# Two interleaved linear-attention and squared-ReLU layers on one core: key sums a tile later, and softmax, weight splits and a norm queued behind the work beside them

## The chip, the cores and the metric

The kernel runs on one core of a Trainium2 chip. The metric is the device time of one launch in microseconds (us). The engines are named as the profile names them: PE (TensorE, matrix products), DVE (VectorE), ACT (ScalarE), POOL (GpSimd), SP (SyncE, which issues the DMAs). Each engine works through one queue in order, so what stands where in a queue decides who waits for whom.

## The reference, cut to what matters

```python
def _A_ref(x, wqkv, w_phi, wo):                   # S=2048, D=576, H=32 heads of 18
    q, k, v = heads of (x @ wqkv)
    pq, pk = q @ w_phi[h], k @ w_phi[h]
    phi_q = concat(softmax(pq), softmax(-pq)); phi_k = concat(softmax(pk), softmax(-pk))
    kv = einsum("bhsf,bhsd->bhfd", phi_k, v); z = phi_k summed over s
    o = (phi_q @ kv) / (phi_q @ z + 1e-6)
    return o (heads joined) @ wo
def _B_ref(x, w1, b1, w2, b2):                    # F=4608
    return relu(x @ w1 + b1) ** 2 @ w2 + b2
x = A_x
for _ in range(2):
    x = x + _A_ref(layernorm(x), ...)
    x = x + _B_ref(layernorm(x), ...)
```

All values are fp32. The key sums kv and z run over all 2048 rows, so no row's attention can end before every row's keys are in.

## The kernel before

The 2048 rows are four blocks of 512 rows, each of four tiles of 128. A product in fp32 is made of three fp32r products: an operand is split into a high part (a copy by ACT) and a low part (a subtraction by DVE, a remainder by POOL). The 4608 hidden columns are 36 groups of 128.

The work is written as generators. `weave` runs one generator and advances a second one beside it by its costs; `pipeline` runs the tiles of a block through a list of stages, later stages of earlier tiles first; a stage `None` or an empty function only delays. The order written is not yet the order of the queues: a scheduler then sorts each engine's instructions by priority. `tc.issue_after(ins)` keeps what is written inside it behind `ins` on that instruction's engine, and `held(gen, keys)` does so for every step of a generator, with the instruction that `dense[key]` names at that moment: "last" is the low part of the newest hidden group (on DVE), "squared" its last square (on ACT).

Each of the two layers runs through these stages:

- Dense layer of the first block (`g_mlp`; names m_3 in the first layer, m_1 in the second), woven with the attention of another block. For each group ACT evicts the hidden product (L812), squares it (L813, L814), and PE adds the previous group's second product. The attention's softmax is `g_features`: maxima and minima on DVE, a difference on POOL (L475), the exponential on ACT (L479), sums and products for the features, scaling. Some queries (`a_1q`, L435, evicted at L453) lie here too.
- Dense layer of the second block (m_2, m_0), woven with the attention of the last two blocks, their norms (`g_norm_first`, `g_norm_second`) and the first weight splits (`prelude`).
- Products of the last two blocks together (`g_pair.products`): 18 pairs of hidden groups, each pair seven products of Strassen's kind instead of eight. In order they are a11, a12, s1, s2, s4, s3, (the second product of an earlier group), a22, another second product. The PSUM tile bx (m_ppx) takes a11, s2, s3 and a22 in one sum, which is read in between: z is the first column group (ACT L1210, DVE L1212, ACT L1213, L1121, L1122, and its low part on DVE L1123), u (DVE L1222, then L1225) and v (ACT L1221, then DVE L1226) belong to the other block and are kept in memory until later. Beside a pair the operands of a coming pair are split (`split_pair`: ACT L1069, DVE L1070, POOL L1072, and POOL's additions L1075 to L1084).
- `seconds`: the second products of the kept block, 36 groups, each fed by a weight split (L1102) and a reload of the kept values (L1187). In the first layer it is woven with `back_keys`, which makes the norm (L344 scales a tile, L355 transposes it, L364 its low part), values, keys, softmax and key sums (`kv_tile`, L527) of three blocks for the second layer. A tile's key sums need the softmax scaled by POOL (L495).

The rest is the start (`g_fold` folds w_phi into the weights, woven with the first norm), the keys of the first layer, and a `barrier` at each layer's start.

Of the kernel before, what the change touches and what calls it, by code (L numbers as in the profile page):

```python
# [21 lines left out]
def layers_kernel(  # L22
# [188 lines left out]
    def g_fold(kpair, vpair):  # L211
# [22 lines left out]
        def turn(k):  # L234
            c, i = divmod(k, 3)
            if i == 0:
                if c + 2 < NC:
                    load(c + 2)
                load_v(c)
                if c in (2, 3):  # L240
                    folds[c] = sb.tile([P, 2 * D], F32, tag="wraw", name=f"ff{c}", bufs=2)
                else:
                    folds[c] = sb.tile([P, 2 * D], F32R, tag="hb", name=f"ff{c}").bitcast(F32)
            w, n = gw[batches[i][0][1]], len(batches[i])
            pt = wtile(f"fp{c}_{i}")
# [4 lines left out]
            nc.vector.tensor_copy(wt[:w, : n * P], pt[:w, : n * P])  # L250
            return wt

        def times(k, wt):
# [414 lines left out]
    def g_features(layer, raws, ph, name):  # L668

        rs, ms = {}, {}  # L670

        def start(t):
            ph.append(soft_parts(raws[t], f"{name}Q{t}"))

        def add(t):
            rs[t] = soft_sums(ph[t], f"{name}Q{t}")
            ms[t] = phi_products(layer, ph[t], f"{name}m{t}")

        def factors(t):
            phi_factors(ms.pop(t), rs[t], f"{name}u{t}")  # L680

        yield from held(pipeline(NT, (start, lambda t: soft_exp(ph[t]), add, factors, lambda t: phi_scale(ph[t], rs[t])),
                                 (2.6, 0.4, 3.0, 2.8, 1.2)))

    def g_out(layer, b, ph, dst, name, parts=1, pause=None, behind=None, norm=None, mid=None, costs=(None, None)):

# [85 lines left out]
    def g_mlp(layer, b, x, after, name, behind=None, then=None):  # L772
# [88 lines left out]
        features(NF - 1, range(3))  # L861
        yt = sb.tile([P, TB], F32, tag="hr", name=f"{name}yt", bufs=2)
        nc.scalar.activation(yt, acc[KC], AF.Copy)
        by_rows(NF - 1, range(2), range(3))
        pt = wtile(f"{name}py")
        p3 = pt.rearrange("p (t d) -> p t d", d=P)
# [2 lines left out]
        for t in range(NT):  # L869
# [1 line left out]
            nc.sync.dma_start(x, xm[b][t])  # L871
            nc.vector.tensor_add(x[:, R:], p3[:, t], x[:, R:])
            after.append(x)
        if then:
            then()
        by_rows(NF - 1, range(2, NT), range(3))
        for t, x in enumerate(after):
            nc.vector.tensor_add(x[:, :R], acc[t][:, :R], x[:, :R])
# [3 lines left out]
    def g_norm_halves(x_of, name, then, main, tail, costs):  # L882
# [35 lines left out]
        def call(pair):  # L918
            def stage(i):
                h, j = divmod(i, 3)  # L920
                pair[j == 2](h if j == 2 else 2 * h + j, pts[i])
# [4 lines left out]
    def g_norm_first(x_of, dst, name, then):  # L926

        tiles = {}

        def main(t, p4):  # L930
            if t == 0:
                tiles.update(xt_tiles(name))
                tiles["t"] = sb.tile([P, 2 * D], F32, tag="E", name=f"{name}t", bufs=4)[:TP, : 2 * TB]
                tiles["t"] = tiles["t"].rearrange("p (a n) -> p a n", a=2)
            rows = slice(t * P, (t + 1) * P)
            hi, lo = tiles["h"][:, :KC, rows], tiles["l"][:, :, rows]
            p3 = p4.rearrange("p a c n -> p (a c) n")
            nc.scalar.activation(hi, p3, AF.Copy)
            nc.vector.tensor_sub(lo, p3, hi.bitcast(F32))

        def tail(h, p3):
            nc.scalar.activation(tiles["t"][:, :, h * TB // 2 : (h + 1) * TB // 2], p3, AF.Copy)

        yield from g_norm_halves(x_of, name, then, (main,), (tail,), (0.3, 1.0))
        nc.sync.dma_start(pth, tiles["h"][:, :KC].rearrange("p c n -> p (c n)").bitcast(F32))
        nc.sync.dma_start(ptl, tiles["l"].rearrange("p c n -> p (c n)").bitcast(F32))
        nc.sync.dma_start(ptt, tiles["t"].rearrange("p a n -> p (a n)"))
# [84 lines left out]
    def g_pair(layer, blocks, x, after, name):  # L1032
# [82 lines left out]
        def bias(f):  # L1115
            return b1t[:, f : f + 1]

        def square(f, r):
            hb = sb.tile([P, 2 * D], F32R, tag="hb", name=f"{name}hb{f}")
            hh, hl = hb[:, :TB], hb[:, TB : 2 * TB]  # L1120
            nc.scalar.activation(hh, r, AF.Square)  # L1121
            nc.scalar.activation(r, r, AF.Square)  # L1122
            nc.vector.tensor_sub(hl, r, hh.bitcast(F32))  # L1123
            high[f] = (hh, hl)

        def features(f, ks):
            b, g = divmod(f, NF)
# [72 lines left out]
        def products():  # L1200
            for k in range(NP):
# [9 lines left out]
                product(k, by, "a12", "b21", True)  # L1211
                nc.vector.tensor_add(z, by, z)  # L1212
                nc.scalar.activation(z, z, AF.Relu)  # L1213
                square(f0, z)
                advance(prep, 2)
                product(k, bz, "s1", "t1", True)
                advance(prep, 2)
                product(k, bx, "s2", "t2", False)
                u = sb.tile([P, D], F32, tag="qk", name=f"{name}u{f0}", bufs=5)[:, :TB]
                v = sb.tile([P, D], F32, tag="qk", name=f"{name}u{f1}", bufs=5)[:, :TB]  # L1220
                nc.scalar.activation(v, bz, AF.Copy)  # L1221
                nc.vector.tensor_add(u, bx, v)  # L1222
                product(k, by, "s4", "b22", True)
                product(k, bx, "s3", "t3", False)
                nc.vector.scalar_tensor_tensor(u, by, bias(f0), u, op0=ALU.add, op1=ALU.add)  # L1225
                nc.vector.scalar_tensor_tensor(v, bx, bias(f1), v, op0=ALU.add, op1=ALU.add)  # L1226
# [4 lines left out]
                if k:  # L1231
                    second(f0 - 1)
                load_wide(f1)
                advance(prep, 2)
                if k == 0:
                    yield
                product(k, bx, "a22", "t4", False)
                drain(prep)
                z = sb.tile([P, TB], F32, tag="hr", name=f"{name}z{f1}", bufs=2)
                nc.scalar.activation(z, bx, AF.Relu, bias=bias(f1))  # L1240
                square(f1, z)
                if k + 2 < NP:
                    raws[k + 2] = load_pair(k + 2)
                if k == 0:
# [80 lines left out]
    xT = [{} for _ in range(NB)]  # L1325
    kpair = [piece_tiles(f"w0k{h}", TAGS_B) for h in range(2)]
    vpair = [piece_tiles(f"w0v{h}", TAGS_A) for h in range(2)]
    weave(g_fold(kpair, vpair), g_norm(load_x(0), xT[0], "n0_0"), 0.5)
    pending = []

    def g_keys(b):
# [21 lines left out]
    for layer in range(2):  # L1353
# [23 lines left out]

        def back_keys():
            new_slots("vs")
            for b in order[:3]:  # L1380
                m = f"1_{b}"
                last = b == order[2]
                xk, vts, raws, es, rs = {}, [], {}, {}, {}
                yield from g_norm(rows_of(b), xk, f"n{m}", fine=True)
                if not last:
                    spill(b, xk)
                    yield from paced(g_v(xk, wpair("v", f"w{m}"), vts, f"v{m}"), 1.0)
# [9 lines left out]
                    rs[t] = soft_sums(es[t], f"k{m}K{t}")  # L1397
                    soft_scale(es[t], rs[t])

                stages = (raw, start, lambda t: soft_exp(es[t]), end, lambda t: None)  # L1400
                if not last:
                    stages += (lambda t: kv_tile(1, vts[t], es[t], f"kv{m}_{t}"),)
                yield from pipeline(NT, stages, (1.0, 2.6, 0.4, 1.8, 0.1, 0.8))
                if last:
                    keep.update(x=xk, es=es, v=wpair("v", f"w{m}"))

# [45 lines left out]
```

## Time and profile before

| what | value |
|---|---|
| median of 3 runs | 2559.05 us (2557.98 to 2560.22) |
| the profiled execution | 2559.82 us, its span 2558.1 us |
| mean granted TensorE clock | 0.988 |
| busy: PE, DVE, ACT, POOL | 2490.5, 1632.0, 1306.9, 967.7 us |
| DMA | 312.99 MB moved, mean 122 GB/s |

The span is the time from the first to the last instruction; 1.7 us of the profiled execution's time lie outside it. Busy times are per engine. A row of waits names the engine and tile that waited, the line, what released it, the total, how often, and the longest. A timeline row has its start, its length, the line, output and inputs, and in brackets the idle time before it with what ended it. A tile is named without its numbers in the profile (m_pu is u or v of any pair, m_ppx is bx); kv_3k<-k_3K3e is block 3, tile 3.

### The profile page before, as it was taken

How to read it: one execution, taken by the hardware profiler on the slowest of the kernel's cores; microseconds unless marked ns; L12 is line 12 of the kernel's file. 1: busy time of each engine (PE TensorE's matmuls, PEld its weight loads, DVE VectorE, ACT ScalarE, POOL GpSimd, SP SyncE). 2: the span in 40 equal slices, each digit the busy share in tenths (PEclk: the TensorE clock that was granted, in tenths of full speed). 3: DMA queues.
4: the chain of work that ended last, by engine and by line, in shares of the span. 5: the costliest groups of instructions: out<-in, count | busy, mean ns of one | idle time of the engine just before them, and what ended most of it. 6: DMA issues, size and time to landing. Idle time of an engine off the chain costs nothing. (4 is left out here: it accounts for less than half of the span.)

```text
span 2558.1 us, 41548 instructions
## 1 busy us (share of the span) xinstructions
PE 2490.5 (97%) x15108; PEld 2188.9 (86%) x15108; DVE 1632.0 (64%) x2570; ACT 1306.9 (51%) x2293; POOL 967.7 (38%) x1101
## 2 busy tenths in 40 slices
PE   8998999999999999999999989999999999999999
PEld 8998888888888888888889988888888887888888
DVE  6778847554966655555777779384658665555444
ACT  4334545354546666664443445553545466666643
POOL 3544313212325555551434433032122445555322
PEclk9998999999999999999999989999999999999999
DMA  8102432345234433338543143233453344333363
GB/s 252 57 23 88 153 92 81 107 144 187 87 116 126 138 117 101 112 102 265 178 129 115 46 138 104 80 93 107 142 175 90 125 129 144 107 103 103 110 201 128
DMA packets 257224, 312.99 MB, mean 122 GB/s; under 512 B 29818, under 2 KB 175482, under 8 KB 254458
## 3 DMA queue, kind: packets, MB, share of 16 engines
q1 hardware_dynamic: 255760, 307.64, 38.5%
q8 instruction: 118, 1.93, 0.3%
q10 hardware_dynamic: 1258, 2.70, 0.3%
q14 instruction: 88, 0.72, 0.1%
HBM read 255.42 MB, written 54.82 MB: 121 GB/s over the span
## 5 line engine op out<-in xcount | busy, mean ns | idle before, releaser
L1103 POOL TENSOR_TENSOR m_ps<-m_pr,m_ps 128x128 fp32r<-128x128 f32 x144 | 120.8, 839 | 319.8 <-ACT m_ps L1101 261.0
L1102 DVE TENSOR_TENSOR m_ps<-m_pr,m_ps 128x448 fp32r<-128x448 f32 x144 | 93.9, 652 | 152.9 <-ACT m_ps L1101 147.3
L1142 PE MATMUL m_pacc<-m_ps,m_phb 128*128 128x448 f32 x864 | 188.5, 366 | 0.0
L1142 PEld LDWEIGHTS m_pacc<-m_ps,m_phb 128*128 128x128 f32 x864 | 162.1, 188 | 18.1
L1101 ACT ACTIVATE m_ps<-m_pr 128x576 fp32r<-128x576 f32 x144 | 97.9, 680 | 132.6 <-issue 87.9
L1142 PE MATMUL m_pacacc<-m_ps,m_phc 128*128 128x448 f32 x648 | 145.7, 369 | 0.0
L1142 PEld LDWEIGHTS m_pacacc<-m_ps,m_phc 128*128 128x128 f32 x648 | 123.2, 190 | 10.1
L1123 DVE TENSOR_TENSOR m_phb<-m_pz,m_phb 128x512 fp32r<-128x512 f32 x72 | 56.5, 785 | 115.8 <-ACT m_pz L1122 114.3
L805 PE MATMUL m_1ph<-t1onh,m_1h 128*128 128x512 f32 (+1 forms) x380 | 100.3, 391 | 2.9 <-ACT m_1hr L812 2.4
L805 PE MATMUL m_3ph<-t0onh,m_3h 128*128 128x512 f32 (+1 forms) x380 | 98.6, 386 | 3.8 <-ACT m_3hr L812 2.4
L832 PE MATMUL m_2acc<-m_2s,m_2hb 128*128 128x448 f32 x432 | 100.1, 365 | 0.0
L832 PE MATMUL m_0acc<-m_0s,m_0hb 128*128 128x448 f32 x432 | 100.0, 365 | 0.0
L832 PE MATMUL m_3acc<-m_3s,m_3hb 128*128 128x448 f32 x432 | 99.7, 366 | 0.0
L832 PE MATMUL m_1acc<-m_1s,m_1hb 128*128 128x448 f32 x432 | 99.5, 365 | 0.0
L805 PE MATMUL m_0ph<-a_0nh,m_0h 128*128 128x512 f32 (+1 forms) x380 | 97.8, 384 | 0.0
L805 PE MATMUL m_2ph<-a_2nh,m_2h 128*128 128x512 f32 (+1 forms) x380 | 97.8, 384 | 0.0
L832 PEld LDWEIGHTS m_2acc<-m_2s,m_2hb 128*128 128x128 f32 x432 | 81.0, 188 | 10.6 <-ACT m_2hb L813 0.2
L832 PEld LDWEIGHTS m_0acc<-m_0s,m_0hb 128*128 128x128 f32 x432 | 81.0, 188 | 10.6 <-ACT m_0hb L813 0.2
L832 PEld LDWEIGHTS m_3acc<-m_3s,m_3hb 128*128 128x128 f32 x432 | 81.0, 188 | 10.6 <-ACT m_3hb L813 0.2
L832 PEld LDWEIGHTS m_1acc<-m_1s,m_1hb 128*128 128x128 f32 x432 | 81.0, 188 | 10.3
L805 PEld LDWEIGHTS m_1ph<-t1onh,m_1h 128*128 128x128 f32 x380 | 70.7, 195 | 17.6 <-ACT m_1hr L812 3.3
L805 PEld LDWEIGHTS m_3ph<-t0onh,m_3h 128*128 128x128 f32 x380 | 69.5, 192 | 17.6 <-ACT m_3hr L812 3.3
(2504 smaller groups left out, 7432.9 us busy)
## 6 DMA issues: line engine op xcount, KB each, us to landing
m_pr<-in_B_w SPq DMA_DIRECT2D x144, 288.0 KB
m_pr<-in_B_w SPq DMA_DIRECT2D x72, 256.0 KB
hd<-m_pu SPq DMA_DIRECT2D x72, 256.0 KB
m_pg<-hd SPq DMA_DIRECT2D x72, 256.0 KB
m_3r<-in_B_w SPq DMA_DIRECT2D x36, 288.0 KB
m_2r<-in_B_w SPq DMA_DIRECT2D x36, 288.0 KB
m_1r<-in_B_w SPq DMA_DIRECT2D x36, 288.0 KB
m_0r<-in_B_w SPq DMA_DIRECT2D x36, 288.0 KB
```

The costliest lines, as they stand in the source:

```text
L805: nc.tensor.matmul(ph[:, cols], a, m, start=(k == 0), stop=(k == len(ops) - 1))
L832: nc.tensor.matmul(acc[t][:, :R], a[:, rows], m, start=(f == 0 and k == 0), stop=(f == NF - 1 and k == 2))
L1101: nc.scalar.activation(s2[:, :D], r2, AF.Copy)
L1102: nc.vector.tensor_sub(s2[:, D : D + R], r2[:, :R], s2[:, :R].bitcast(F32))
L1103: nc.gpsimd.tensor_sub(s2[:, D + R : 2 * D], r2[:, R:], s2[:, R:D].bitcast(F32))
L1123: nc.vector.tensor_sub(hl, r, hh.bitcast(F32))
L1142: nc.tensor.matmul(accs[b][t][:, :R], a[:, rows], m, start=(g == 0 and k == 0), stop=(g == NF - 1 and k == 2))
```

## The change

- Key sums: in `back_keys` the last stage puts a tile's key sums in a list and writes those of the tile before it; the last tile's are written after the next block's norm has been written. The delaying stage is taken out.
- Softmax: `g_features` is held behind "last" and "squared" instead of "last" alone, so the exponentials on ACT stand behind the newest square.
- First norm: `g_norm_first` gets an empty stage between transposes and split.
- Products: the low part of z and the four steps of `split_pair` are written after v's copy and u's addition and held behind both; the last two steps are held behind v's addition.
- Dense layer: `then()`, which ends the woven work and writes pair 0 up to s3, comes ahead of the last rows of the second block's dense layer instead of amid them.
- The first two steps of `back_keys` are written in the last pair of the products (first layer).
- The first norm in the fold is held behind the newest copy of `g_fold`.

```diff
@@ g_features
     yield from held(pipeline(NT, (start, lambda t: soft_exp(ph[t]), add, factors, lambda t: phi_scale(ph[t], rs[t])),
-                                 (2.6, 0.4, 3.0, 2.8, 1.2)))
+                                 (2.6, 0.4, 3.0, 2.8, 1.2)), ("last", "squared"))
@@ g_mlp
         nc.scalar.activation(yt, acc[KC], AF.Copy)
+        if then:
+            then()
         by_rows(NF - 1, range(2), range(3))
...
-        if then:
-            then()
         by_rows(NF - 1, range(2, NT), range(3))
@@ g_norm_first
-        yield from g_norm_halves(x_of, name, then, (main,), (tail,), (0.3, 1.0))
+        yield from g_norm_halves(x_of, name, then, (main, None), (tail, None), (0.3, 1.0, 1.0))
@@ g_pair, square
-            nc.vector.tensor_sub(hl, r, hh.bitcast(F32))
             high[f] = (hh, hl)
+            return lambda: nc.vector.tensor_sub(hl, r, hh.bitcast(F32))
@@ g_pair, products
-                square(f0, z)
-                advance(prep, 2)
+                low = square(f0, z)
                 product(k, bz, "s1", "t1", True)
-                advance(prep, 2)
                 product(k, bx, "s2", "t2", False)
...
-                nc.scalar.activation(v, bz, AF.Copy)
-                nc.vector.tensor_add(u, bx, v)
+                copied = nc.scalar.activation(v, bz, AF.Copy)
+                added = nc.vector.tensor_add(u, bx, v)
+                with tc.issue_after(added.ins), tc.issue_after(copied.ins):
+                    low()
+                    advance(prep, 4)
                 product(k, by, "s4", "b22", True)
                 product(k, bx, "s3", "t3", False)
                 nc.vector.scalar_tensor_tensor(u, by, bias(f0), u, op0=ALU.add, op1=ALU.add)
-                nc.vector.scalar_tensor_tensor(v, bx, bias(f1), v, op0=ALU.add, op1=ALU.add)
+                added = nc.vector.scalar_tensor_tensor(v, bx, bias(f1), v, op0=ALU.add, op1=ALU.add)
...
-                advance(prep, 2)
+                with tc.issue_after(added.ins):
+                    advance(prep, 2)
@@ fold
-    weave(g_fold(kpair, vpair), g_norm(load_x(0), xT[0], "n0_0"), 0.5)
+    weave(g_fold(kpair, vpair), held(g_norm(load_x(0), xT[0], "n0_0"), ("folded",)), 0.5)
@@ back_keys
                 yield from g_norm(rows_of(b), xk, f"n{m}", fine=True)
+                while late:
+                    kv_tile(1, *late.pop(0))
+                    yield 0.8
...
-                stages = (raw, start, lambda t: soft_exp(es[t]), end, lambda t: None)
-                if not last:
-                    stages += (lambda t: kv_tile(1, vts[t], es[t], f"kv{m}_{t}"),)
-                yield from pipeline(NT, stages, (1.0, 2.6, 0.4, 1.8, 0.1, 0.8))
+                def keep_sums(t):
+                    if not last:
+                        late.append((vts[t], es[t], f"kv{m}_{t}"))
+                        if len(late) > 1:
+                            kv_tile(1, *late.pop(0))
+
+                yield from pipeline(NT, (raw, start, lambda t: soft_exp(es[t]), end, keep_sums),
+                                    (1.0, 2.6, 0.4, 1.8, 0.8))
@@ the layer
-        drain(products)
+        back = iter(()) if layer else back_keys()
+        for k, _ in enumerate(products):
+            if k == NP - 1:
+                next(back, None)
+                next(back, None)
         spare["tags"] = ["acc4"]
-        weave(seconds, iter(()) if layer else back_keys(), 4.0)
+        weave(seconds, back, 4.0)
```

In `g_pair` most lines of the changed kernel carry a number one higher, so the same split is L1070 before and L1071 after.

PE's queue in `seconds`, where block 3's key sums end: kv1_3_2k and kv1_3_3k are the key sums of tiles 2 and 3, ps2_47 a group of the second matrix. Before:

```order
L1132 MATMUL m0_pacacc3_11966<-m0_phc47_12606,m0_ps2_47_12600 128x512 x3
L527 MATMUL kv1_3_2k_12824<-k1_3K2e_12592,vs2_12028 32x2x18 x32
L527 MATMUL kv1_3_3k_12858<-k1_3K3e_12662,vs3_12029 32x2x18 x32
L1142 MATMUL m0_pach_11962<-m0_ps2_48_12670,m0_phc48_12676 128x448 x3
L1142 MATMUL m0_pacacc0_11963<-m0_ps2_48_12670,m0_phc48_12676 128x448 x3
```

The same place in the changed kernel, up to the first transposes of the next block's norm (n1_2p0, p1, p40):

```order
L527 MATMUL kv1_3_2k_12798<-k1_3K2e_12566,vs2_11922 32x2x18 x32
L1143 MATMUL m0_pach_12001<-m0_ps2_47_12638,m0_phc47_12644 128x448 x3
L1143 MATMUL m0_pacacc0_12002<-m0_ps2_47_12638,m0_phc47_12644 128x448 x3
L1143 MATMUL m0_pacacc1_12003<-m0_ps2_47_12638,m0_phc47_12644 128x448 x3
L1143 MATMUL m0_pacacc2_12004<-m0_ps2_47_12638,m0_phc47_12644 128x448 x3
L1133 MATMUL m0_pacacc3_12005<-m0_phc47_12644,m0_ps2_47_12638 128x512 x3
L355 MATMUL n1_2p0_12885<-ident_149,n1_2n0_12843 128x128 x4
L355 MATMUL n1_2p1_12894<-ident_149,n1_2n1_12856 128x128 x4
L369 MATMUL n1_2p40_12901<-ident_149,n1_2e_12832 128x128 x2
```

Groups 48 and 49 follow there, and then, word for word, the place to which tile 3 has moved:

```order
L355 MATMUL n1_2p2_12984<-ident_149,n1_2n2_12942 128x128 x4
L355 MATMUL n1_2p3_12991<-ident_149,n1_2n3_12955 128x128 x4
L369 MATMUL n1_2p41_12998<-ident_149,n1_2e_12832 128x128 x2
L1143 MATMUL m0_pach_12001<-m0_ps2_50_12861,m0_phc50_12867 128x448 x3
L1143 MATMUL m0_pacacc0_12002<-m0_ps2_50_12861,m0_phc50_12867 128x448 x3
L527 MATMUL kv1_3_3k_13003<-k1_3K3e_12662,vs3_11923 32x2x18 x32
```

Tile 3's key sums moved from right behind tile 2's to behind three groups, both sets of the norm's transposes and a part of a fourth group. Tiles 0 to 2 keep a group between them in this block; in the next one tiles 0 and 1 follow each other.

DVE's queue in pair 8 of the products: pz16 is z, phb16 its low part, pu16 and pu17 are u and v, pwv, pwa, pwb and pwc are weight splits. Before:

```order
L1212 TENSOR_TENSOR m0_pz16_10363<-m0_ppy8_10348,m0_pz16_10363 128x512
L1070 TENSOR_TENSOR m0_pwv1_10_10544<-m0_pr1_10_10487,m0_pwv1_10_10544 128x256
L1123 TENSOR_TENSOR m0_phb16_10374<-m0_pz16_10363,m0_phb16_10374 128x512
L1222 TENSOR_TENSOR m0_pu16_10412<-m0_ppx8_10347,m0_pu17_10413 128x512
L1070 TENSOR_TENSOR m0_pwv2_10_10545<-m0_ps0_10_10539,m0_pwv2_10_10545 128x256
L1225 SCALAR_TENSOR_TENSOR m0_pu16_10412<-m0_ppy8_10348,b1t_184,m0_pu16_10412 128x512
L1070 TENSOR_TENSOR m0_pwv3_10_10546<-m0_ps1_10_10540,m0_pwv3_10_10546 128x256
L1070 TENSOR_TENSOR m0_pwa_10_10541<-m0_pr1_10_10487,m0_pwa_10_10541 128x256
L1070 TENSOR_TENSOR m0_pwa_10_10541<-m0_pr0_10_10481,m0_pwa_10_10541 128x256
L1226 SCALAR_TENSOR_TENSOR m0_pu17_10413<-m0_ppx8_10347,b1t_184,m0_pu17_10413 128x512
```

The same stretch of the changed kernel, in its own line numbers (L1221 is u's addition, L1125 the low part, L1227 and L1228 the last additions to u and v):

```order
L1213 TENSOR_TENSOR m0_pz16_10363<-m0_ppy8_10348,m0_pz16_10363 128x512
L1071 TENSOR_TENSOR m0_pwb_10_10560<-m0_pr1_10_10487,m0_pwb_10_10560 128x256
L1221 TENSOR_TENSOR m0_pu16_10391<-m0_ppx8_10347,m0_pu17_10392 128x512
L1125 TENSOR_TENSOR m0_phb16_10374<-m0_pz16_10363,m0_phb16_10374 128x512
L1071 TENSOR_TENSOR m0_pwc_9h_10398<-m0_pr0_9_10320,m0_pwc_9h_10398 128x256
L1071 TENSOR_TENSOR m0_pwc_9h_10398<-m0_pr1_9_10326,m0_pwc_9h_10398 128x256
L1071 TENSOR_TENSOR m0_pwc_9h_10398<-m0_ps0_9_10396,m0_pwc_9h_10398 128x256
L1071 TENSOR_TENSOR m0_pwc_9h_10398<-m0_ps1_9_10397,m0_pwc_9h_10398 128x256
L1227 SCALAR_TENSOR_TENSOR m0_pu16_10391<-m0_ppy8_10348,b1t_184,m0_pu16_10391 128x512
L1228 SCALAR_TENSOR_TENSOR m0_pu17_10392<-m0_ppx8_10347,b1t_184,m0_pu17_10392 128x512
```

The addition to u moved ahead of the low part, and four splits in a row now stand between u's addition and the last additions; the splits are those of the next pair, where before they were of the pair after it.

ACT's queue in the first dense layer (m_3): hr21 to hr25 are hidden groups, a0_0Q3e the fourth exponential of the attention beside it. Before:

```order
L813 ACTIVATE m0_3hb21_4985<-m0_3hr21_4984 128x512
L814 ACTIVATE m0_3hr21_4984<-m0_3hr21_4984 128x512
L791 ACTIVATE m0_3s2_22_4963<-m0_3r2_22_4957 128x576
L479 ACTIVATE a0_0Q3e_5006<-a0_0Q3e_5006 128x1152
L812 ACTIVATE m0_3hr22_5040<-m0_3ph22_4969,b1t_184 128x512
```

In the changed kernel the same exponential stands here:

```order
L812 ACTIVATE m0_3hr24_5154<-m0_3ph24_5083,b1t_184 128x512
L790 ACTIVATE m0_3h1_26_5191<-m0_3r1_26_5185 128x640
L813 ACTIVATE m0_3hb24_5155<-m0_3hr24_5154 128x512
L814 ACTIVATE m0_3hr24_5154<-m0_3hr24_5154 128x512
L479 ACTIVATE a0_0Q3e_5006<-a0_0Q3e_5006 128x1152
L791 ACTIVATE m0_3s2_25_5133<-m0_3r2_25_5127 128x576
```

It moved from ahead of the eviction of group 22 to behind the squares of group 24.

More of the change, by code (lines that the diff above doesn't have):

```diff
@@ L249, in turn @@
             wt = sb.tile([GW, TB], F32R, tag="ft", name=f"ft{c}_{i}", bufs=4).bitcast(F32)
-            nc.vector.tensor_copy(wt[:w, : n * P], pt[:w, : n * P])
+            dense["folded"] = nc.vector.tensor_copy(wt[:w, : n * P], pt[:w, : n * P])
             return wt
@@ L920, in stage @@
                 h, j = divmod(i, 3)
-                pair[j == 2](h if j == 2 else 2 * h + j, pts[i])
+                if pair[j == 2]:
+                    pair[j == 2](h if j == 2 else 2 * h + j, pts[i])
             return stage
@@ L1240, in products @@
                 nc.scalar.activation(z, bx, AF.Relu, bias=bias(f1))
-                square(f1, z)
+                square(f1, z)()
                 if k + 2 < NP:
@@ L1379, in back_keys @@
             new_slots("vs")
+            late = []
             for b in order[:3]:
```

## The prediction

> **What bounds the kernel now.** I read the page's busy times first, then the list of what TensorE (PE) waits for, then the granted clock in windows around the longest waits, and last the timelines of the engines that PE waits for.
>
> ```profile
> PE 2490.5 (97%) x15108; PEld 2188.9 (86%) x15108; DVE 1632.0 (64%) x2570; ACT 1306.9 (51%) x2293; POOL 967.7 (38%) x1101
> core 0: 2558.1 us, clock 0.988
> ```
>
> PE is busy for 2490.5 of 2558.1 us, so all that an edit of order can win is its idle time, 67.6 us, and the time it works at a reduced clock. Everything else has spare time on average. The waits tell where (line waited for: us in total, times, longest us):
>
> ```profile
> PE kv_3k L527 <- POOL k_3K3e L495: 6.1, 1, 6.1
> PE kv_3k L527 <- POOL k_2K3e L495: 5.0, 1, 5.0
> PE m_ppx L1113 <- DVE m_pu L1226: 2.8, 2, 1.4
> PE m_1ph L805 <- ACT m_1hr L812: 2.4, 1, 2.4
> PE m_3ph L805 <- ACT m_3hr L812: 2.4, 1, 2.4
> PE n_3p L355 <- DVE n_3n L344: 2.4, 1, 2.4
> PE a_1qp L435 <- ACT a_1qs L453: 1.6, 1, 1.6
> PE a_2qp L435 <- ACT a_2qs L453: 1.6, 1, 1.6
> ```
>
> The edits touch each of these rows. A wait also costs after it has ended. The next rows are windows of PE (time, length, busy with matmul count, granted clock): after the two key-sum waits, and after the m_1ph wait. Above them stand the last key sums of a block, waited for, and one that wasn't.
>
> ```profile
> 1322.43 0.77 PE L527 MATMUL kv_2k<-k_2K2e,vs 128*32 128x36 f32 x64
> 1328.24 1.19 PE L527 MATMUL kv_3k<-k_2K3e,vs 128*32 128x36 f32 x64 [5.04 <-POOL k_2K3e L495]
> 1252.37 1.19 PE L527 MATMUL kv_3k<-k_3K3e,vs 128*32 128x36 f32 x64 [6.05 <-POOL k_3K3e L495]
> ...
> 1253.00:1257.00 4.00, 4.00 (x52) 0.70 0.61 196
> 1330.00:1334.00 4.00, 4.00 (x13) 0.51 0.85 277
> 1698.00:1704.00 6.00, 6.00 (x21) 0.72 0.36 104
> ```
>
> PE was busy throughout, but at a clock of 0.70, 0.51 and 0.72. The work lost is 4 x 0.30 = 1.2, 4 x 0.49 = 2.0 and 6 x 0.28 = 1.7 us, and each waited-for group of key sums took 1.19 instead of 0.77, 0.8 for both: 5.7 us in all. The Trainium skill ("TensorE: Matmul & The Clock Gate", Part 1: The HAM clock gate) says that the clock falls to one half only after at least one idle window of about 3.4 us. By that rule the 2.4 us wait of m_1ph would cost no clock and my sum would win 1.7 us less; the window from 1698 on, at 0.72 behind just such a wait, speaks against it, and the measurement decides.
>
> **Key sums one tile later.** POOL's last scaling ends at 1249.99 + 2.33 = 1252.3, when PE has waited since 1246.3.
>
> ```profile
> 1249.99 2.33 POOL L495 TENSOR_TENSOR k_3K3e<-k_3K3e,k_3K3r 128x1152 f32<-128x1152 f32 x1 [2.54 <-DVE k_3K3r L484]
> ...
> 1254.56 0.45 DVE L535 TENSOR_TENSOR kv<-kv_3k,kv 128x288 f32<-128x288 f32 x1
> 1258.21 0.55 DVE L344 TENSOR_SCALAR n_2n<-x,n_2m,n_2d 128x512 f32<-128x512 f32 x1 [3.20 <-PE n_2p L355]
> 1261.27 0.54 DVE L344 TENSOR_SCALAR n_2n<-x,n_2m,n_2d 128x512 f32<-128x512 f32 x1
> ...
> 1257.57 1.04 PE L355 MATMUL n_2p<-ident,n_2n 128*128 128x128 f32 x8
> ```
>
> The key sums of tile 3 now stand behind three groups of the second matrix and two sets of transposes, over 11 us later, so both waits go: 6.05 + 5.04 = 11.1, and 1.2 + 2.0 + 0.8 = 4.0 of clock. What is late next? DVE was behind too: without a pause it comes to 1254.6, and only then scales the third tile of the next norm; the fourth follows 3.6 us later (1261.27 + 0.54 against 1258.21), and L377, 0.4, now lies between, so it is there at 1254.6 + 4.0 = 1258.6. PE, not stopped at 1246.3, does three groups of 3.16 (worked out below), the transposes, some 1.2, and half a set, 0.5: it wants that tile at 1257.4. A new wait of 1.3 on n_2p, bounded by 0 and the 6.1 it replaces. In the next block DVE and POOL are no further behind and the norm there comes one group later, so I put none. Of the key sums' own earlier tiles none is nearer to its scaling than before.
>
> **Softmax behind "last" and "squared".** An exponential at the head of ACT's queue waits for POOL or DVE while the eviction that PE needs is behind it.
>
> ```profile
> 432.47 1.16 ACT L479 ACTIVATE a_0Q3e<-a_0Q3e 128x1152 f32<-128x1152 f32 x1 [6.21 <-POOL a_0Q3e L475]
> 433.54 0.67 ACT L812 ACTIVATE m_3hr<-m_3ph,b1t 128x512 f32<-128x512 f32 x1
> ...
> 649.24 1.16 ACT L479 ACTIVATE a_1Q1e<-a_1Q1e 128x1152 f32<-128x1152 f32 x1 [3.56 <-POOL a_1Q1e L475]
> 650.31 0.39 ACT L453 ACTIVATE a_1qs<-a_1qp 128x288 f32<-128x288 f32 x1
> ```
>
> L812 came at 433.54 because the exponential waited 6.21 for POOL. It now stands three hidden groups later, by when POOL is done. That returns 2.4 + 2.4 = 4.8, the 1.7 of clock behind the second, and 1.6 + 1.6 = 3.2 in the queries. The price is that the held block's attention runs about one hidden group later: its transposes and norm may wait for an engine. The nearest row is a wait of 1.6; between 0 and that I take 1 us a layer, 2.0. The operands of pair 0 come out of the same queue; they still end before the last groups of the dense layer, which cover them.
>
> **Products: low parts and splits behind the additions.** In a pair, DVE adds u (L1222) after the low part of z (L1123), which waits for ACT; the product s3 waits for u's addition. The first two rows are one pair on DVE; then come all pairs but the first of each layer (count, minimum/median/maximum ns, first and last start), and the first product of pair 5, the second one and the next pair's.
>
> ```profile
> 996.58 1.03 DVE L1123 TENSOR_TENSOR m_phb<-m_pz,m_phb 128x512 fp32r<-128x512 f32 x1 [2.03 <-ACT m_pz L1122]
> 997.53 0.68 DVE L1222 TENSOR_TENSOR m_pu<-m_ppx,m_pu 128x512 f32<-128x512 f32 x1
> ...
> L1222 DVE TENSOR_TENSOR m_pu<-m_ppx,m_pu x17: 677/683/687, 872.6 to 1157.2; 128x512 f32<-128x512 f32 x17
> L1222 DVE TENSOR_TENSOR m_pu<-m_ppx,m_pu x17: 677/684/687, 2137.8 to 2425.7; 128x512 f32<-128x512 f32 x17
> ...
> 936.50 0.62 PE L1113 MATMUL m_ppx<-a_1nb11h,m_pwc_5h 128*128 128x512 f32 x2
> 938.11 0.62 PE L1113 MATMUL m_ppy<-a_1nb21h,m_pwc_5h 128*128 128x512 f32 x2
> 954.09 0.62 PE L1113 MATMUL m_ppx<-a_1nb11h,m_pwv 128*128 128x512 f32 x2
> 2203.54 0.62 PE L1113 MATMUL m_ppx<-a_2nb11h,m_pwc_5h 128*128 128x512 f32 x2
> 2221.33 0.62 PE L1113 MATMUL m_ppx<-a_2nb11h,m_pwv 128*128 128x512 f32 x2
> ```
>
> The mean pair is (1157.2 - 872.6) / 16 = 17.79, a pair without a wait 954.09 - 936.50 = 17.59: 0.20 x 16 = 3.2 us. In the second layer 17.99 against 17.79, 3.2 again. With u first this goes: 6.4. But v's addition (L1226, now L1228) is then behind u's addition, the low part, four splits and L1225, and the product a22 waits for it. A product is 938.11 - 936.50 = 1.61, so a group is (17.59 - 7 x 1.61) / 2 = 3.16, and from s4's start to a22's lie 2 x 1.61 + 3.16 = 6.38; u can begin some 0.2 into it. A row on DVE overlaps its follower by 0.08 (997.53 + 0.68 ends at 998.21, its follower has begun by then), so u, low part, L1225, v are 0.60 + 0.61 (0.95 when slow) + 0.66 + 0.74 = 2.6 to 3.0.
>
> ```profile
> L1123 DVE TENSOR_TENSOR m_phb<-m_pz,m_phb x72: 684/693/1036, 854.3 to 2435.3; 128x512 fp32r<-128x512 f32 x72
> L1225 DVE SCALAR_TENSOR_TENSOR m_pu<-m_ppy,b1t,m_pu x36: 736/739/753, 856.4 to 2426.9; 128x512 f32<-128x512 f32 x36
> ...
> L1070 DVE TENSOR_TENSOR m_pwv<-m_pr,m_pwv x36: 414/418/1240, 813.8 to 2369.1; 128x256 fp32r<-128x256 f32 x36
> L1070 DVE TENSOR_TENSOR m_pwv<-m_ps,m_pwv x36: 418/684/1232, 816.7 to 2374.3; 128x256 fp32r<-128x256 f32 x36
> ...
> 980.33 1.76 DVE L1070 TENSOR_TENSOR m_pwc_9h<-m_pr,m_pwc_9h 128x256 fp32r<-128x256 f32 x2
> 980.20 1.01 POOL L1078 TENSOR_TENSOR m_ps<-m_ps,m_pr 128x384 f32<-128x384 f32 x1
> ```
>
> That leaves 6.18 - 3.0 = 3.2 for four splits, 0.80 each, or 0.88 as a row shows it. Most splits of a loaded operand take 0.42; the two at 980.33, beside a POOL addition, took (1.76 + 0.08) / 2 = 0.92 each; the longest 1.24. All at 0.42 no wait, all at 0.92 a wait of 0.14, all at 1.24 one of 1.4. POOL's four additions come in the same stretch now, so I go by 0.92 and take 0.1: 34 x 0.1 = 3.4 given back.
>
> **Pair 0.** The last rows of the dense layer move behind the product s3, so PE has their 1.5 to 2 us to do while DVE makes v: the 2.8 of L1226 goes, unless v is later there too.
>
> **What is worth nothing.** The first norm's empty stage moves two tiles' transposes behind a group; the key sums' first steps now start in the last pair, which brings a load and its statistics ahead. The n_3p wait of 2.4 hangs on a later tile, so between 0 and 2.4 I take 0. Holding the first norm in the fold leaves the order of every engine there as it was: 0.
>
> **The sum.** Won: 11.1 + 4.0 + 4.8 + 1.7 + 3.2 + 6.4 + 2.8 = 34.0. Given back: 1.3 + 2.0 + 3.4 = 6.7. Net 27.3. The profiled execution took 2559.8 (span 2558.1), the median is 2559.05: 2559.05 - 27.3 = 2531.7.
>
> **The rivals.**
> - Waits move instead of going. The exponentials and the norms are only put later; DVE is behind at 1254. Against it: after the key sums DVE idles 3.20 us. If half of the 11.1 and of its 4.0 of clock returns, and one 1.6 a layer more, the net is 27.3 - (5.5 - 1.3) - 2.0 - 1.2 = 19.9: 2539. Chance 0.17.
> - Only the key sums pay: 11.1 + 4.0 - 1.3 = 13.8, the softmax and pair terms cancelling against later waits: 2545. Chance 0.10.
> - Slower: v's addition becomes the bound of every pair. It decides when four splits average over 0.88; at 1.12 each the wait is 4 x 1.04 - 3.2 = 0.96, x 34 = 33, and all is lost; at the longest row, 1.24, it is 1.4 x 34 = 48 against 34.0 - 3.3 = 30.7: 2576. For it: POOL adds in the same stretch. Against it: no median of the rows above is over 0.92. Chance 0.07. The Trainium skill ("GPSIMD Engine Reference", 1. Specifications) says that POOL's SBUF interfaces are shared with VectorE, with contention for DVE instructions of two SBUF inputs. A split is such an instruction, so by that rule alone all four go at the slow price of 0.92, which is 0.14 a pair, 4.8 in place of 3.4; the rows' 0.42 in the median and 0.92 beside POOL agree with it.
> - The rows that PE waits for are not the true releasers and nothing moves: 2559. Chance 0.04.
>
> **How the numbers follow.** My forecast has 0.62, at 2531.7, and by its own bounds (nothing given back and n_3p too; all splits slow and both attentions late by 1.6 more) it lies between 2522 and 2537. To hold 8 in 10 the range reaches over the first rival and most of the second: 2522 to 2547. This kernel can be told from no change from about 0.2%, 5.1 us. Faster by more: 0.62 + 0.17 + 0.10 = 0.89; within: 0.04; slower: 0.07.
>
> **What would show it.** In the profile after: no wait of kv_3k and no window under 0.9 behind it; no m_3ph or m_1ph wait on L812; a mean pair near 17.7 and 17.9; a new n_2p wait near 1.3. I am wrong if PE waits for L1228 in most pairs, if the key-sum wait stands under another name at its old size, or if the held softmax makes the last dense block wait before pair 0.

## The result and the profile after

The changed kernel took 2563.6 us in the median (2560.1 to 2566.2, 11 runs) beside 2559.5 us of the kernel before (2554.9 to 2562.1, 11 runs): a ratio of 1.002, 95% interval 1.0012 to 1.0029. The forecast was 2531.7, the range 2522 to 2547. It is slower by 4 us where 27 fewer were forecast.

From the page, and below it the mean granted clock:

```profile
PE 2496.9 (97%) x15108; PEld 2180.4 (85%) x15108; DVE 1651.9 (64%) x2570; ACT 1295.8 (51%) x2293; POOL 953.0 (37%) x1101
core 0: 2562.3 us, clock 0.991
```

What PE waits for, of the rows that are new:

```profile
PE m_ppx L1114 <- DVE m_pu L1221: 8.5, 13, 1.3
PE m_ppx L1114 <- DVE m_pu L1228: 6.8, 18, 0.5
...
PE n_2p L369 <- DVE kv L535: 2.6, 1, 2.6
...
PE m_pacc L1143 <- DVE m_2x L878: 1.6, 3, 0.8
...
PE n_2p L355 <- DVE kv L535: 1.2, 1, 1.2
...
PE kv_3k L527 <- DVE n_2l L364: 0.5, 1, 0.5
```

The waits of 6.1 and 5.0 us for the key sums, both 2.4 us waits for L812 and both 1.6 us waits of the queries are gone, as forecast. In their place the products wait for both additions, u's (L1221) and v's (L1228), 31 times, 15.3 us in all; before it was 5 times and 4.7 us.

The start times of a few PE instructions cut both traces into stages (us; the stretches left out differ by 0.1 in all):

| stage | before | after | difference |
|---|---|---|---|
| up to the first dense block | 256.5 | 255.0 | -1.5 |
| first dense blocks (m_3, m_1) | 282.6 + 287.6 | 277.7 + 283.0 | -9.5 |
| second dense blocks and pair 0 | 326.3 + 326.4 | 325.1 + 325.6 | -2.0 |
| pairs 1 to 17 | 298.9 + 302.3 | 313.1 + 312.1 | +24.0 |
| second products, first layer, with the key sums | 215.7 | 210.2 | -5.5 |
| from there to the second layer | 129.4 | 128.1 | -1.3 |

Everything outside the pairs won 19.8 us; the pairs lost 24.0. The rows of u's addition give the mean pair (pairs 1 to 17, first and last start, one layer in each):

```profile
L1221 DVE TENSOR_TENSOR m_pu<-m_ppx,m_pu x17: 690/692/692, 864.6 to 1163.4; 128x512 f32<-128x512 f32 x17
L1221 DVE TENSOR_TENSOR m_pu<-m_ppx,m_pu x17: 690/691/692, 2131.6 to 2429.5; 128x512 f32<-128x512 f32 x17
```

(1163.4 - 864.6) / 16 = 18.68 and, in the second layer, 18.62, against 17.79 and 17.99 before.

The even pairs show why. First ACT in pair 12, then DVE, then PE:

```profile
1064.31 0.69 ACT L1211 ACTIVATE m_pz<-m_ppx,b1t 128x512 f32<-128x512 f32 x1
1068.90 0.53 ACT L1070 ACTIVATE m_pwb<-m_pr 128x384 fp32r<-128x384 f32 x1 [3.90 <-DMA m_pr<-in_B_w]
1069.33 0.62 ACT L1214 ACTIVATE m_pz<-m_pz 128x512 f32<-128x512 f32 x1
...
1070.52 0.58 ACT L1220 ACTIVATE m_pu<-m_ppz 128x512 f32<-128x512 f32 x1
...
1071.13 0.69 DVE L1221 TENSOR_TENSOR m_pu<-m_ppx,m_pu 128x512 f32<-128x512 f32 x1 [1.25 <-ACT m_pu L1220]
...
1072.33 1.84 DVE L1071 TENSOR_TENSOR m_pwc_13h<-m_pr,m_pwc_13h 128x256 fp32r<-128x256 f32 x2
1074.09 1.83 DVE L1071 TENSOR_TENSOR m_pwc_13h<-m_ps,m_pwc_13h 128x256 fp32r<-128x256 f32 x2
...
1076.51 0.74 DVE L1228 SCALAR_TENSOR_TENSOR m_pu<-m_ppx,b1t,m_pu 128x512 f32<-128x512 f32 x1
...
1068.95 0.85 PE L1114 MATMUL m_ppy<-a_1nh,m_pwa 128*128 128x512 f32 x3
...
1071.87 0.73 PE L1114 MATMUL m_ppx<-a_1nt3h,m_pwa 128*128 128x512 f32 x2 [1.15 <-DVE m_pu L1221]
...
1077.31 0.50 PE L1114 MATMUL m_ppx<-a_1nt4h,m_pwb 128*128 128x512 f32 x1 [0.39 <-DVE m_pu L1228]
```

In the middle of z's chain, between L1211 and L1214, ACT has a split of the a22 operand of pair 14 (m_pwb). It waits 3.90 us for its load. Behind it stand the rest of z, v's copy (L1220) and so u's addition, s3, the four splits, v's addition and a22: one wait is paid twice on PE, 1.15 and 0.39, since the chain from u to v is longer than PE's work between them. A row of waits counts only PE's idle time. By the starts of s4, s3 and a22 the pair loses more: 1071.87 - 1068.95 = 2.92 where a product is 1.61, and 1077.31 - 1071.87 = 5.44 where a product and a group are 4.77, so 1.3 and 0.7. That is why the waits above don't make up the 24.0 by themselves.

The load is late because SP waits for the buffer. SP's waits in pairs 1 to 17 of the first layer, the changed kernel and then the kernel before; then ACT's waits for the load in the same order:

```profile
SPq L1045 <- DVE m_pwa L1071: 62.6, 7, 9.6
...
SPq L1044 <- DVE m_pwa L1070: 36.4, 6, 6.4
...
ACT m_pwb L1070 <- DMA m_pr<-in_B_w: 23.9, 7, 4.1
...
ACT m_pwb L1069 <- DMA m_pr<-in_B_w: 2.0, 4, 0.8
```

The raw operands (m_pr) of pair 14 go into the tiles that pair 12's operands leave, and these are free when pair 12's last split (m_pwa) has read them. The change moved that split to behind the additions of pair 11. ACT waited 2.0 us in 4 pairs before, 23.9 in 7 after.

### The profile page after: what moved, and what is told of

Same layout as the page of the kernel before. It is cut to its first block, busy times and chain, and to the rows that moved or that the text cites. A ratio compares the mean times of both kernels' runs of the same rounds, so it can differ in the third digit from the quotient of the medians.

```text
span 2562.3 us, 41566 instructions
## 1 busy us (share of the span) xinstructions
PE 2496.9 (97%) x15108; PEld 2180.4 (85%) x15108; DVE 1651.9 (64%) x2570; ACT 1295.8 (51%) x2293; POOL 953.0 (37%) x1101
## 5 line engine op out<-in xcount | busy, mean ns | idle before, releaser
L832 PEld LDWEIGHTS m_0acc<-m_0s,m_0hb 128*128 128x128 f32 x432 | 80.9, 188 | 10.6 <-ACT m_0hb L813 0.2
L795 POOL TENSOR_TENSOR m_1s<-m_1r,m_1s 128x128 fp32r<-128x128 f32 x36 | 25.0, 695 | 148.5 <-ACT m_1s L791 142.3
```

The costliest lines, as they stand in the source:

```text
L832: nc.tensor.matmul(acc[t][:, :R], a[:, rows], m, start=(f == 0 and k == 0), stop=(f == NF - 1 and k == 2))
```

## The experiments

"Ratio" is always to the kernel before, run beside on the same chip.

**The products edit out, and the products edit alone.** The first kernel is the changed one with these lines as before, the second the one before with these lines as after:

```diff
-                low = square(f0, z)
+                square(f0, z)
+                advance(prep, 2)
                 product(k, bz, "s1", "t1", True)
+                advance(prep, 2)
...
-                with tc.issue_after(added.ins), tc.issue_after(copied.ins):
-                    low()
-                    advance(prep, 4)
...
-                with tc.issue_after(added.ins):
-                    advance(prep, 2)
+                advance(prep, 2)
```

> The changed kernel with the products stage as it was before (low part, splits and u's addition in the old order), all other edits kept. In the traces the two products stages took 14.2 and 9.8 us longer after the change and the rest of the program 19.8 us less. If that split is a sum of independent parts: 2563.6 - 24.0 = about 2540, 0.992 of the kernel before. If the other edits also lengthen the products stage (earlier start of the key-sum steps, later attention): 2545 to 2560.

> The kernel before with the products edit alone. If the edit costs its 24 us by itself: about 2583, 1.0094 of the kernel before, with the wait of the a22 split for its load in the even pairs. If the loss needs the other edits: between 2555 and 2570.

Without it: 2535.8 us, ratio 0.9909 (0.9892 to 0.9926). Alone: 2592.8 us, ratio 1.0131 (1.0113 to 1.015). So the rest of the change wins 22.8 us, and the products edit loses 27.8 on top of the rest, 34.2 by itself. Three of the four executions of the second kernel show a mean clock of 0.986 to 0.987 and take 2592 to 2596 us, the fourth 0.991 and 2586.2, so a part of the 34.2 is clock. Both the 22.8 and the 27.8 are somewhat more than the stage table gave: the edit also cost the pair 0 stage 3.9 us (325.1 + 325.6 against 323.4 + 323.4 without it).

**The a22 split held too.**

```diff
-                drain(prep)
+                with tc.issue_after(added.ins), tc.issue_after(copied.ins):
+                    drain(prep)
```

> The changed kernel with one more hold: the last split of a pair's operands (a22) also stands behind that pair's copy of v on ACT and its addition to v on DVE. Theory 1, the loss comes from the a22 split of the even pairs, which stands at the head of ACT's queue and waits up to 4 us for a load that is issued later now: that wait goes, u comes in time, and what is left is about 0.13 us a pair for v; two times 10 us less, 2540 to 2545. Theory 2, the loss is the chain on DVE itself, u, low part, four splits beside POOL's additions, L1227, L1228: nothing of that changes, 2558 to 2564.

2541.5 us, ratio 0.9936 (0.9921 to 0.9951). The mean pair is (1154.5 - 867.1) / 16 = 17.96 and 17.91, so theory 1 holds and most of the loss came by way of that one split:

```profile
L1221 DVE TENSOR_TENSOR m_pu<-m_ppx,m_pu x17: 690/692/693, 867.1 to 1154.5; 128x512 f32<-128x512 f32 x17
L1221 DVE TENSOR_TENSOR m_pu<-m_ppx,m_pu x17: 690/692/693, 2120.2 to 2406.8; 128x512 f32<-128x512 f32 x17
```

Is a late load enough by itself? The next rows are the last loads of an operand pair on SP and the L1211 beside them, first in the changed kernel (4.45 us is eight issues), then with a22 held:

```profile
1062.97 4.45 SPq L1047 DMA_DIRECT2D m_pr<-in_B_w  x8
...
1059.59 1.85 SPq L1047 DMA_DIRECT2D m_pr<-in_B_w  x4
...
1058.68 0.69 ACT L1211 ACTIVATE m_pz<-m_ppx,b1t 128x512 f32<-128x512 f32 x1 [0.29 <-PE m_ppx L1114]
```

The last issue ends at 1067.4, 3.1 behind L1211's start at 1064.31, and at 1061.4, 2.8 behind 1058.68. The load is about as late with a22 held; nobody waits, for the split that needs it stands later in ACT's queue. With the next run, where the split stands ahead and the load is in time, this shows that the loss takes both: the late load and the split ahead of z's relu.

**Only u's addition first, the splits where they were.**

```diff
                 low = square(f0, z)
+                advance(prep, 2)
                 product(k, bz, "s1", "t1", True)
+                advance(prep, 2)
...
                     low()
-                    advance(prep, 4)
...
-                with tc.issue_after(added.ins):
-                    advance(prep, 2)
+                advance(prep, 2)
```

> The changed kernel with only the low part held behind u's addition; the splits are written where they were before and not held. Both theories: no late u and no row of four splits, so the products stage is at or below the time before, the whole at 2534 to 2541. If POOL's additions and the splits of the pair after next collide with the low part in its new place: above 2545.

2528.9 us, ratio 0.9886 (0.9872 to 0.9901): the products at (1142.8 - 861.2) / 16 = 17.60 and 17.79 a pair, which is the pair without a wait.

```profile
L1223 DVE TENSOR_TENSOR m_pu<-m_ppx,m_pu x17: 690/692/692, 861.2 to 1142.8; 128x512 f32<-128x512 f32 x17
L1223 DVE TENSOR_TENSOR m_pu<-m_ppx,m_pu x17: 690/692/693, 2109.9 to 2394.5; 128x512 f32<-128x512 f32 x17
...
ACT m_pwb L1070 <- DMA m_pr<-in_B_w: 3.2, 5, 1.2
```

The a22 split stands at the same place here, but its load comes in time: SP's waits for m_pwa are back at 36.4 us, those of ACT for the load at 3.2. Of the edit to the products the one step "u before the low part" is the good one, 2535.8 - 2528.9 = 6.9 us, and the splits behind it are the bad one. All later kernels start from this one.

**Two of the four splits behind v** (on top of a22_held).

```diff
-                    advance(prep, 4)
+                    advance(prep, 2)
...
                 with tc.issue_after(added.ins):
-                    advance(prep, 2)
+                    advance(prep, 4)
```

> The run a22_held with two of the four splits moved from ahead of v's additions to behind them on DVE; ACT's order is the same. If the rest of the loss against u_first_only (2541.5 against 2528.9) is v's wait for the four splits beside POOL's additions: the product a22 starts without a wait, 0.15 us a pair is won, 5 us in all: 2535 to 2538. If it is the six splits in a row on ACT, which wait for POOL and hold the eviction of z and so the next pair's first product: within 2 us of a22_held, 2540 to 2543.

2542.5 us, ratio 0.9939 (0.9924 to 0.9954): no gain, the time of the second reading. v's addition came in time (no row of m_ppx waiting for L1228 is left), and from s3's start to a22's PE took 3.3 us less over all pairs, so that wait was real; but PE waits elsewhere:

```profile
PE m_pacc L1143 <- DVE m_2x L878: 3.0, 2, 2.2
...
PE m_ppx L1114 <- ACT m_pz L1244: 2.5, 4, 1.3
...
1066.93 0.94 ACT L1070 ACTIVATE m_pwc_13l<-m_pr 128x384 fp32r<-128x384 f32 x2 [1.23 <-POOL m_pr L1082]
1069.76 0.53 ACT L1070 ACTIVATE m_pwc_13l<-m_pr 128x384 fp32r<-128x384 f32 x1 [1.89 <-POOL m_pr L1085]
...
1073.14 0.67 ACT L1244 ACTIVATE m_pz<-m_ppx,b1t 128x512 f32<-128x512 f32 x1
```

The splits in a row on ACT wait for one POOL addition after another, 1.23 and 1.89 us, and so the eviction of a22's result (L1244) comes late for the next pair's a11. In pair 0 the last rows' additions of the dense layer (L878) stand behind the splits on DVE, and the second products wait for their PSUM tiles: the second dense blocks with pair 0 took 2.1 and 3.0 us more than with a22_held.

**The softmax without its hold**, and **the key sums as before** (each from u_first_only).

```diff
-                                 (2.6, 0.4, 3.0, 2.8, 1.2)), ("last", "squared"))
+                                 (2.6, 0.4, 3.0, 2.8, 1.2)))
```

```diff
-                while late:
-                    kv_tile(1, *late.pop(0))
-                    yield 0.8
...
-                yield from pipeline(NT, (raw, start, lambda t: soft_exp(es[t]), end, keep_sums),
-                                    (1.0, 2.6, 0.4, 1.8, 0.8))
+                stages = (raw, start, lambda t: soft_exp(es[t]), end, lambda t: None)
+                if not last:
+                    stages += (lambda t: kv_tile(1, vts[t], es[t], f"kv{m}_{t}"),)
+                yield from pipeline(NT, stages, (1.0, 2.6, 0.4, 1.8, 0.1, 0.8))
```

> The run u_first_only without the hold of the softmax. The first dense blocks took 4.9 and 4.6 us less in the changed kernel; the prediction gave this edit 4.8 + 1.7 + 3.2 - 2.0 = 7.7. Expected 2536 to 2539. If the hold only shifted the waits: within 3 us of 2528.9.

> The run u_first_only with the key sums' edit undone. The stage of the second products took 5.5 us less in the changed kernel, where the prediction gave this edit 11.1 + 4.0 - 1.3 = 13.8. By the stage table 2533 to 2536; by the prediction 2541 to 2544. The waits of kv_3k, 6.1 and 5.0 us, should be back and those of n_2p gone.

Softmax: 2544.9 us, ratio 0.9948 (0.9933 to 0.9963), 16.0 more. The old waits are back, and with them one in each second dense block that neither trace had shown:

```profile
PE m_1ph L805 <- ACT m_1hr L812: 2.4, 1, 2.4
PE m_3ph L805 <- ACT m_3hr L812: 2.4, 1, 2.4
...
PE m_2ph L805 <- ACT m_2hr L812: 1.9, 1, 1.9
```

By its trace the dense blocks account for 15.0 of the 16.0: 7.8 in the first ones, 7.2 in the second ones, where the queries' waits lie too.

Key sums: 2534.6 us, ratio 0.9905 (0.9889 to 0.9922), 5.7 more, with the waits of kv_3k back at 6.5 and 3.8 us and none of n_2p. The stage table was right, the forecast's 13.8 was not.

**The norm two groups later, and one group later.** The waits of n_2p are for DVE's addition L535. Rows of the changed kernel:

```profile
1255.03 0.46 DVE L535 TENSOR_TENSOR kv<-kv_1k,kv 128x288 f32<-128x288 f32 x1
...
1258.26 0.44 DVE L535 TENSOR_TENSOR kv<-kv_2k,kv 128x288 f32<-128x288 f32 x1
...
1255.55 0.66 PE L355 MATMUL n_2p<-ident,n_2n 128*128 128x128 f32 x4 [1.18 <-DVE kv L535]
1258.76 0.69 PE L369 MATMUL n_2p<-ident,n_2e 128*128 128x128 f32 x2 [2.56 <-DVE kv L535]
```

Each transpose begins when an addition has ended (1255.49, 1258.70): three PSUM tiles rotate there, and the transposes take those that the key sums of tiles 1 and 2 held. Before, PE stood still for tile 3 meanwhile.

```diff
+                if b == order[1]:        # u_norm_one; u_norm_later: if late: yield 8.0
+                    yield 4.0
                 yield from g_norm(rows_of(b), xk, f"n{m}", fine=True)
```

> The run u_first_only with the norm of the next block written two groups of the second matrix later in back_keys. The transposes n_2p waited 1.2 + 2.6 us because their PSUM tiles were those of tiles 1 and 2 of the key sums, which DVE had not yet added (L535), and the clock fell behind that. If that is the cause: both waits and the fall of the clock behind them go, 4 to 7 us: 2522 to 2525, 0.9862 of the kernel before. If the tile waits for DVE's scaling, as the prediction had it, the wait only moves by two groups: 2527 to 2531.

> The run u_first_only with the second norm of back_keys alone one group of the second matrix later (u_norm_later moved two norms by two groups, won 8.4 us within the stage and gave 7.9 back behind it, where a wait of 5.4 us stood for want of cover). If the tiles of the key sums are the cause and one group is enough: the waits of n_2p fall from 3.8 us to under 1 and the clock holds, and with six groups left behind the keys nothing is given back: 2523 to 2526. If any shift is paid for at the end: 2528 to 2530.

Two norms by two groups: 2529.6 us, ratio 0.989 (0.9875 to 0.9905), no gain; the waits of n_2p are gone, but behind the stage PE waits 5.4 us for ACT, it seems for want of groups to cover the end:

```profile
PE m_ppy L1160 <- ACT m_pyt L1155: 5.4, 1, 5.4
```

One norm by one group: 2526.0 us, ratio 0.9871 (0.9857 to 0.9886), the best kernel here; its interval overlaps that of u_first_only (0.9872 to 0.9901), so the times alone don't part the two. Its trace speaks for a gain: the stage took 205.4 instead of 210.1, of n_2p 0.8 us is left, though kv_3k waits 1.2 more; 1.7 of the difference is one fall of the clock less.

**The pair's start back amid the last rows, and the edits put at nothing.** The first moves `then()` back, the second takes out the empty stage of the first norm, the early start of the key-sum steps and the hold in the fold.

```diff
-        if then:
-            then()
         by_rows(NF - 1, range(2), range(3))
...
+        if then:
+            then()
         by_rows(NF - 1, range(2, NT), range(3))
```

```diff
-        yield from g_norm_halves(x_of, name, then, (main, None), (tail, None), (0.3, 1.0, 1.0))
+        yield from g_norm_halves(x_of, name, then, (main,), (tail,), (0.3, 1.0))
...
-    weave(g_fold(kpair, vpair), held(g_norm(load_x(0), xT[0], "n0_0"), ("folded",)), 0.5)
+    weave(g_fold(kpair, vpair), g_norm(load_x(0), xT[0], "n0_0"), 0.5)
...
-        for k, _ in enumerate(products):
-            if k == NP - 1:
-                next(back, None)
-                next(back, None)
+        drain(products)
```

> The run u_first_only with the pair's start back amid the dense layer's last rows. The prediction gave this edit 2.8 us, the wait of the first a22 for v: 2531 to 2533. If the u-first order alone has taken that wait away: 2528 to 2530.

> The run u_first_only without the three edits that were put at nothing: the empty stage in the first norm, the early start of the key-sum steps, the hold in the fold. If they are worth nothing: 2527 to 2531. If the empty stage spares waits in the second dense block, or the early start gives the next stage its cover: 2532 to 2537.

2531.6 us, ratio 0.9894 (0.9878 to 0.9911): 2.6 more, as forecast. And 2529.9, ratio 0.9886 (0.9871 to 0.99): 0.9 more, within the noise and as forecast, but not for the reason given. In its trace the second dense blocks with pair 0 are 2.1 and 1.8 longer, because the queries' wait is back (it lies there, not in the first dense block), and the key-sum stage is 4.6 shorter. PE's waits in that trace:

```profile
PE a_2qp L435 <- ACT a_2qs L453: 1.6, 1, 1.6
PE a_1qp L435 <- ACT a_1qs L453: 1.6, 1, 1.6
```

Two effects of opposite sign stood behind the zero, so it came out by luck. Of the 4.6, 3.4 is clock: in u_first_only it fell to one half for 3.41 us twice in that stage, here never, and the last section shows that this hangs on where a wait happens to lie. The queries' wait is back in u_no_softmax as well: it goes only with the softmax hold and one of these three edits together (which one was not tested), where the prediction gave it to the hold alone.

## Why the prediction was wrong

By its steps, in us won (each measured as the kernel without that edit against u_first_only, or as said):

| term | forecast | measured |
|---|---|---|
| u before the low part | 6.4 | 6.9 (2535.8 - 2528.9) |
| weight splits behind the additions | -3.4 | -34.7 (2528.9 - 2563.6) |
| softmax hold | 4.8 + 1.7 + 3.2 - 2.0 = 7.7 | 16.0 |
| key sums, with their clock | 11.1 + 4.0 - 1.3 = 13.8 | 5.7 |
| pair 0 | 2.8 | 2.6 |
| the rest | 0 | 0.9 |

**The step that failed** is "low parts and splits behind the additions". It followed the four splits on DVE and took 0.1 us a pair. But a split is more than its DVE instruction. It also frees the raw operand's buffer; SP waits for that before it can load the pair after next; and of those operands one split, a22's, was not held and stood a pair early on ACT, ahead of z's relu. I had the wait of ACT for that load in the trace before (2.0 us in 4 waits of one layer) and did not follow what a later load does to it. The runs show its price: 22.1 us (2563.6 - 2541.5).

PE's time between the starts of a pair's products, summed over pairs 1 to 17 of both layers (us; the last line to pair 16), shows where it goes:

| from, to | u_first_only | a22_held | changed kernel |
|---|---|---|---|
| a11, s4 | 221.3 | 221.9 | 223.0 |
| s4, s3 (waits for u) | 55.5 | 55.5 | 66.1 |
| s3, a22 (waits for v) | 162.0 | 165.2 | 174.2 |
| a22, next a11 (waits for ACT's eviction) | 153.2 | 157.1 | 159.1 |

The chain from the end of u's addition to that of v's takes 5.4 to 5.5 us in pairs 1 to 15 of both kernels, but for one pair. u's addition ends about 0.95 us after s4's start in every pair of a22_held, and 1.6 to 3.1 us after it in the even pairs 2 to 14 of the changed kernel. With u in time the chain costs 3.3 us at a22, just what was forecast for it (3.4): that price was right. With u late the same chain costs 12.3, and u itself 10.6. The other 12.6 of the 34.7 (2541.5 - 2528.9) are, by the two traces, these 3.3, another 3.9 behind a22, where ACT's row of splits waits for POOL and holds the eviction back, and 4.6 in the second dense blocks with pair 0, where the additions L878 are late; 0.8 is left.

**The rival "v's addition becomes the bound"** and its sign, waits for L1228 in most pairs (18 such waits came), had the right place and missed the cause. It was to decide when four splits average over 0.88; they took (1.84 + 0.08) / 2 = 0.96 in pair 12, over that point. By that rival's own reckoning 0.96 costs 4 x 0.88 - 3.2 = 0.3 us a pair; 12.3 / 34 = 0.36 was lost at a22, but only because u came late, and 0.1 when it did not.

**The key sums**: the engine and the place were right, the releaser and the size were not. I named DVE as late and forecast a wait of 1.3 for the fourth tile's scaling (by its own figures 1258.6 - 1257.4 = 1.2); the waits that came, 1.2 + 2.6, are for PSUM tiles that DVE's additions L535 release, two instructions of the same queue. And the clock fell all the same: in the changed kernel it is at 0.59 over the 8 us behind them.

```profile
1258.00:1266.00 8.00, 7.24 (x23) 0.59 0.83 282
```

PE was busy for 7.24 of them: 7.24 x 0.41 = 3.0 us of clock still paid, of the 4.0 that were to be won.

**The softmax hold** won twice what was forecast. Its own delay, put at 2.0, cost nothing that shows. A kernel without it also waits in the second dense blocks, 1.9 and 1.8 us. The kernel before has no hold and not these waits, so they come with the other edits; with which, and how, was not tested.

One slip in the sum is too small to matter: four splits at 0.92 give a wait of 4 x 0.04 = 0.16, not 0.14.

The range failed because the price of the splits was bounded only by rows of DVE. The queues that the moved step also feeds, SP and ACT, had no term.

## What to carry to other kernels

A step that is moved takes with it what it releases. For each operand read, ask which load waits for that buffer, who needs that load first, and whether this reader stands ahead of something urgent in its own queue; a hold on some of a group of instructions leaves the others to be sorted ahead of them. And before several edits are put together, try the smallest part of each: here one moved subtraction carried all that the products had to give.

## What the runs showed of the hardware

The clock did not follow the length of a wait. The same wait, 2.6 us of n_2p for L535, in the runs u_first_only and u_no_rest, two windows of 4 us each from the wait on, first of the one run and then of the other (start:end, length, busy with count, granted clock):

```profile
1236.00:1240.00 4.00, 1.44 (x9) 1.00 0.19 33
1240.00:1244.00 4.00, 4.00 (x13) 0.57 1.01 366
...
1240.00:1244.00 4.00, 2.19 (x12) 1.00 0.49 157
1244.00:1248.00 4.00, 4.00 (x21) 1.00 0.97 330
```

The first lost 4 x 0.43 = 1.7 us of clock behind the wait, the second none. A shorter wait, 1.2 and 0.8 us, lies 0.7 us ahead of each. Inside the traces a fall of the clock lasts 3.41 us or a multiple of it, and the falls of one trace start whole multiples of 3.41 apart, so these traces can be cut into the windows by which the clock goes (in u_no_rest from the fall at 1448.28, 61 windows behind 1240.07). Cut so, the same two runs:

```profile
1233.51:1236.92 3.41, 1.82 (x12) 1.00 0.70 219
1236.92:1240.34 3.42, 1.21 (x7) 1.00 0.27 63
1240.34:1243.75 3.41, 3.41 (x11) 0.50 1.01 359
...
1236.66:1240.07 3.41, 1.82 (x12) 1.00 0.57 195
1240.07:1243.48 3.41, 1.67 (x9) 1.00 0.44 143
1243.48:1246.89 3.41, 3.41 (x18) 1.00 0.99 334
```

In the first run one window holds 3.42 - 1.21 = 2.2 us of idle time, and the next runs at 0.50. In the second the waits are shared out as 1.6 and 1.7 over two windows, and nothing falls. In the traces of all kernels here, from 30 us on, each of the 72 windows at full clock with 2.0 us or more of idle time was followed by one at half clock, and none of the 9268 with less than 1.5; of the 58 between, 14 were.

The Trainium skill ("TensorE: Matmul & The Clock Gate", Part 1: The HAM clock gate) says that activity is judged in free-running windows of about 3.4 us, and that agrees: the same wait costs clock or not by where it falls. That the fall needs a whole idle window does not agree with the first run, where no idle time was over 2.6 us.
